# A fused attention and two feed-forwards: token chunks of 512, 384, 512, 512, 384 columns instead of 512 and four of 448, a 96-byte pad first on SBUF's right side, and attention paced anew

## The chip, the cores and the metric

One core of a Trainium2 chip. The time is that of the device for one execution, in microseconds. Five engines work side by side: TensorE (PE, matmuls; PEld is its weight load), VectorE (DVE), ScalarE (ACT), GpSimd (POOL) and SyncE (SP, which issues the DMAs).

## The reference

Attention over 4 batches, 8 heads, 576 positions of 64; heads 0 to 3 look at a window of 32 positions, heads 4 to 7 at every 32nd position. Then a feed-forward with a gate (512 to 1536 and back), then a second one that takes the largest of three products (512 to 768 and back).

```python
mask_local = (rel >= 0) & (rel < 32)
mask_strided = (rel >= 0) & (pos[None, :] % 32 == pos[:, None] % 32)
scores = np.where(masks, q @ k.T / np.sqrt(64), -1e9)       # heads 0-3 local, 4-7 strided
attn = np.exp(scores - scores.max(-1)); attn /= attn.sum(-1) + 1e-9
x = (attn @ v)                                              # 2304 tokens x 512
g = x @ w_gate
x = (g * (1.0 / (1.0 + np.exp(-g))) * (x @ w_val)) @ w_out  # first feed-forward
out = np.maximum(np.maximum(x @ w1, x @ w2), x @ w3) @ w_out2
```

## The kernel before

The 2304 tokens are 72 rows of 32 positions (18 rows to a batch). `ROWS` cuts them into five chunks; a chunk's width is 32 times its rows, and `width(c)` is the number of columns of every matmul of the first feed-forward for it. Rows 16 and 17 come last (`ORDER`).

*First feed-forward.* For each chunk c and each f of 12 there is a slot: `emit_gate` (12 matmuls into `ps_g`, a Silu on ACT, L717), `emit_val` (12 into `ps_v`, the multiply `ht` on DVE, L724, then its high part `hh` on ACT, L730, and its low part `hl` on POOL, L734) and `emit_out` of the slot before (12 into `ps_y`). `product` (L696 to L700) multiplies fp32 as three passes of a high and a low part: 36 wide matmuls to a slot. `ps_g` and `ps_v` share two banks of the pool `gv`. The weights `w_v` and `w_o` are read again from DRAM for every chunk but the first (`reload`, three buffers each), `w_g` stays in SBUF.

*Attention.* A chunk's attention is done while the chunk before it is in the feed-forward. The local heads go through PE in blocks of 64 queries (`Block`: scores L390, softmax on DVE and ACT, transposes L459, outputs L501); two blocks are done as a pair (`scores_with`, `outputs_with`), each having claimed its banks with a tiny ACT instruction (`claimed`, L306). A row group that has no neighbour in the chunk is a block with a single one. The strided heads of batch 0 (16 rows) and of batch 1's first 14 rows (`ON_PE`) go through PE as well (`strided_block`); the other rows are a `Unit` on DVE: a product over all keys and a sum (L597, L600) for each row's scores, exp on ACT (L607), a product and a sum for its outputs (L619, L622), and transposes on PE (L629). `attention_steps(c)` lays a chunk's attention out in 15 steps, which are called in the slots from three before to eleven after the beginning of chunk c - 1 (L1067 to L1072); a `Unit` takes four steps.

*Second feed-forward's weights.* In 60 steps (`pair_steps`, L256) the weights of the second feed-forward are loaded, rounded, combined and written to DRAM in the form in which they are used, with work on ACT, DVE and POOL. `PACE[c]` says how many of these steps a slot of chunk c takes, in the first ten slots of a chunk.

*Order of the work.* Chunk 0's feed-forward and chunk 1's attention are put in order by hand (`FIRST`: a letter for the kind of step, a number for the block, weight or f). From chunk 1 to slot 9 of chunk 4 the scheduler of the tile framework orders the instructions of each engine, and each engine works in that order. From slot 10 of chunk 4 on (the seam) the order is that of the code again: the loads and splits of `y` for the second feed-forward (`load_y`, `some`), the last two slots, and then the second feed-forward (L855), whose matmuls have 384 columns.

*SBUF.* The pools of the left side (`x`, `h`, weights, four of the second feed-forward's five weight buffers) and those of the right side (attention's tiles, `raw`, the strided keys and products; later `y`, its combinations `r` and one weight buffer) grow from both ends. In this kernel the tiles of the right side begin 96 bytes past a multiple of 128; those of the left side at multiples of 128.

Of the kernel before, what the change touches and what calls it, by code (L numbers as in the profile page):

```python
# [64 lines left out]
u4 B4 d14 V10 w4 c15 r20 s15 c16 t15 q16 s16 h14 y12 d15 P10 a17 o14 q17 O3 x4 c17 H10 l12 h15 t16 r23 s17 L10
z4 d16 E11 y13 o15 G5 h16 j4 q18 R11 m12 l13 m13 o16 a18 r24 s18 N11 t17 c18 a19 T11 d17 S12 u5 y15 t18 c19 B5
V11 w5 h17 M12 q19 r22 o17 a20 d18 E12 t19 s20 P11 y16 x5 G6 c20 h18 R12 H11 t20 z5 N12 s19 L11 r26 j5 q20 T12
o18 a21 O4 d20 r25 V12 d19 q21 h20 c21 h19 o20 r27 s21 t21 P12 S13 o19 a22 B6 d21 H12 l14 l15 u6 c22 L12 y19
h21 s22 w6 q22 o21 q23 r28 t22 O5 a24 x6 s23 c24 m14 m15 d22 z6 y18 q24 s24 h22 j6 a23 o22 G7 r29 a25 M13 c23
q25 t24 E13 r31 t23 c25 d24 W14 s25 d23 y21 B7 h24 R13 M14 h23 N13 u7 y22 o23 E14 w7 t25 T13 M15 r32 a26 o24  # L70
O6 V13 R14 s26 x7 q26 c26 r30 a27 N14 z7 t26 q27 d25 P13 r33 a28 j7 G8 h25 d26 H13 o25 s27 L13 c27 y24 h26 c28
t27 a29 T14 o26 q29 r34 B8 d27 V14 s28 u8 s29 c29 w8 y25 t28 h27 q28 t29 o27 a30 O7 r35 x8 s30 q30 d28 z8 y27
c30 h28 j8 a31 o28 q31 G9 d29 q32 y28 s31 c31 t30 h29 t31 E15 d30 O8 d31 u9 o29 h30 R15 h31 o30 a32 N15 y30
a33 w9 B9 s32 q33 o31 a34 c32 y31 q34 c33 s33 t32 T15 a35 x9 c34 G10 V15 t33 s34 z9 d32 q35 j9 h32 d33 s35 P14
# [1176 lines left out]
```

## Time and profile before

| | |
|---|---|
| time, median of 3 runs | 789.13 us (787.82 to 789.27) |
| profiled execution: span | 789.6 us |
| PE / DVE / ACT / POOL busy | 774.2 (98%) / 612.6 (78%) / 400.7 (51%) / 229.8 us (29%) |
| chunk 0 (25.90 to 143.40) | 117.50 us, DVE busy 110.48 |
| chunk 1 (143.40 to 240.30) | 96.90 us, DVE busy 78.04 |
| chunk 2 (240.30 to 336.50) | 96.20 us, DVE busy 88.03 |
| chunk 3 (336.50 to 430.20) | 93.70 us, DVE busy 84.02 |
| chunk 4 (430.20 to 518.00) | 87.80 us, DVE busy 64.91 |
| second feed-forward (518.00 to 789.60) | 271.60 us, DVE busy 172.58 |

The profile is of one execution. Busy times are sums of the durations of an engine's instructions in a stretch; an engine that is busy for the whole of one sets its length, if what it does is needed. The rows are in the section after the next. Line numbers are those of the kernel before; in the changed one the lines from L121 on stand two further down, those behind `attention_steps` four.

### The profile page before, as it was taken

The page shows a single profiled execution, that of the slowest core. Times are in us where ns is not written, and L with a number is a line of the kernel's source. Part 1 is how long each engine was busy: PE and PEld are TensorE (multiplying, and loading weights), DVE is VectorE, ACT ScalarE, POOL GpSimd, SP SyncE. Part 2 cuts the span into 40 slices and gives each one's busy share as a digit, 9 for nine tenths or more (in the row PEclk, how much of TensorE's full clock was granted, in tenths as well). Part 3 has the DMA queues.
Part 4 walks back from the last instruction along what each step waited for, and adds up shares of the span by engine and source line. Part 5 has one row for each costly group of instructions (what it writes and reads, how often), then busy time and mean ns, then how long its engine had stood idle before and what let it go on. Part 6 is the DMA issues. An engine that isn't in the chain of part 4 may idle for free.

```text
span 789.6 us, 13321 instructions
## 1 busy us (share of the span) xinstructions
PE 774.2 (98%) x4642; PEld 712.0 (90%) x4642; DVE 612.6 (78%) x1206; ACT 400.7 (51%) x925; POOL 229.8 (29%) x225
## 2 busy tenths in 40 slices
PE   6899999999999999999999999999999999999998
PEld 4677788889898998988999999999999999999998
DVE  4899999888959999799795778745689377856683
ACT  6899998554553636545342645433245233443331
POOL 1533343012221432424242646521124011321120
PEclk9899999999999999999999999999999999999999
DMA  9998896977656886747788999996775976878722
GB/s 273 315 316 290 309 356 217 383 255 252 205 202 202 302 294 221 269 169 251 254 277 288 311 387 378 346 370 249 274 265 195 418 258 244 285 285 343 271 94 81
DMA packets 75595, 216.26 MB, mean 274 GB/s; under 512 B 8488, under 2 KB 42024, under 8 KB 70920
## 3 DMA queue, kind: packets, MB, share of 16 engines
q1 hardware_dynamic: 75528, 215.41, 76.9%
q8 instruction: 37, 0.61, 0.3%
q14 instruction: 30, 0.25, 0.1%
HBM read 171.34 MB, written 44.04 MB: 273 GB/s over the span
## 4 chain that ended last, share of the span: by engine, by line
PE 82%; DVE 12%; ACT 3%; issue 2%; DMA 1%; SPq 0%; DVEq 0%; ACTq 0%
PE ps_a L855 19%; PE ps_c L855 10%; PE ps_v L698 5%; PE ps_y L698 5%; PE ps_y L699 5%; PE ps_v L700 5%; PE ps_v L699 5%; PE ps_y L700 5%; PE ps_g L698 5%; PE ps_g L700 5%; PE ps_b L855 5%; PE ps_g L699 5%; DVE pr L619 2%; PE ps_a L501 1%; PE ps_a L459 1%
## 5 line engine op out<-in xcount | busy, mean ns | idle before, releaser
L734 POOL TENSOR_TENSOR hl<-ht,hh 128x448 fp32r<-128x448 f32 x47 | 61.0, 1297 | 213.6 <-ACT hh L730 194.8
L866 ACT ACTIVATE s<-ps_a 128x384 f32<-128x384 f32 x99 | 48.4, 489 | 135.0 <-PE ps_a L855 135.0
L698 PE MATMUL ps_v<-xh,w_v 128*128 128x448 f32 (+1 forms) x240 | 90.8, 378 | 0.9 <-DVE ht L724 0.7
L698 PE MATMUL ps_g<-xh,wh_g 128*128 128x448 f32 (+1 forms) x240 | 90.4, 377 | 0.0
L699 PE MATMUL ps_g<-xl,wh_g 128*128 128x448 f32 (+1 forms) x240 | 89.9, 375 | 0.4 <-DVE xl L519 0.4
L700 PE MATMUL ps_g<-xh,wl_g 128*128 128x448 f32 (+1 forms) x240 | 89.8, 374 | 0.0
L699 PE MATMUL ps_y<-hl,w_o 128*128 128x448 f32 (+1 forms) x240 | 89.6, 373 | 0.0
L700 PE MATMUL ps_y<-hh,w_o 128*128 128x448 f32 (+1 forms) x240 | 89.3, 372 | 0.0
L700 PE MATMUL ps_v<-xh,w_v 128*128 128x448 f32 (+1 forms) x240 | 89.2, 371 | 0.0
L699 PE MATMUL ps_v<-xl,w_v 128*128 128x448 f32 (+1 forms) x240 | 88.9, 370 | 0.0
L698 PE MATMUL ps_y<-hh,w_o 128*128 128x448 f32 (+1 forms) x240 | 83.6, 376 | 0.0
L730 ACT ACTIVATE hh<-ht 128x448 fp32r<-128x448 f32 (+1 forms) x60 | 35.2, 587 | 90.1 <-DVE ht L724 82.8
L805 POOL TENSOR_TENSOR rT<-t,rT 128x384 f32<-128x384 f32 x9 | 12.5, 1390 | 149.3 <-DVE rT L804 149.3
L855 PE MATMUL ps_a<-y0hT,wr 128*128 128x384 f32 x162 | 54.9, 339 | 0.0
L855 PE MATMUL ps_a<-y1hT,wr 128*128 128x384 f32 x162 | 54.5, 337 | 0.0
L698 PEld LDWEIGHTS ps_v<-xh,w_v 128*128 128x128 f32 x240 | 45.1, 188 | 7.0 <-DVE ht L724 1.3
L699 PEld LDWEIGHTS ps_g<-xl,wh_g 128*128 128x128 f32 x240 | 45.4, 189 | 5.5 <-DVE xl L519 0.7
L698 PEld LDWEIGHTS ps_g<-xh,wh_g 128*128 128x128 f32 x240 | 45.3, 189 | 5.6 <-DVE ht L757 0.3
L700 PEld LDWEIGHTS ps_g<-xh,wl_g 128*128 128x128 f32 x240 | 45.4, 189 | 5.1
L698 PEld LDWEIGHTS ps_y<-hh,w_o 128*128 128x128 f32 x240 | 45.1, 188 | 5.2
L897 DVE TENSOR_TENSOR s<-ps_c,s 128x384 f32<-128x384 f32 x36 | 20.0, 556 | 38.2 <-ACT s L866 32.5
L700 PEld LDWEIGHTS ps_y<-hh,w_o 128*128 128x128 f32 x240 | 45.1, 188 | 5.1 <-DVE w_o L248 0.3
(256 smaller groups left out, 2102.1 us busy)
## 6 DMA issues: line engine op xcount, KB each, us to landing
wr<-wsdr SPq DMA_DIRECT2D x36, 1792.0 KB, 8.3
raw<-in_w_dram SPq DMA_DIRECT2D x60, 512.0 KB, 6.8
w_v<-wvdr SPq DMA_DIRECT2D x48, 512.0 KB, 4.2
w_o<-wodr SPq DMA_DIRECT2D x48, 512.0 KB, 4.8
wsdr<-whi SPq DMA_DIRECT2D x36, 256.0 KB, 3.6
wvdr<-w_v SPq DMA_DIRECT2D x12, 512.0 KB, 4.5
wodr<-w_o SPq DMA_DIRECT2D x12, 512.0 KB, 6.1
wsdr<-w SPq DMA_DIRECT2D x24, 256.0 KB, 4.0
```

The source lines that it names most:

```text
L459: nc.tensor.transpose(ps[:sm.shape[2], g * 128:(g + 1) * 128], sm[:, g], ident)
L501: ins = nc.tensor.matmul(ps[j * D:(j + 1) * D, at:at + nq], v, p, start=True, stop=True).ins
L619: eng.tensor_tensor(pv, self.v[:, :, 0:i + 1], self.sc[:, r:r + 1, 0:i + 1].to_broadcast([128, D, i + 1]), ALU.mult)
L698: nc.tensor.matmul(ps, wh, xh, start=first, stop=False)
L699: nc.tensor.matmul(ps, wh, xl, start=False, stop=False)
L700: nc.tensor.matmul(ps, wl, xh, start=False, stop=last)
L730: return nc.scalar.activation(hs[c, f][0], t, AF.Copy).ins
L734: return eng.tensor_tensor(hl, t, f32(hh), ALU.subtract).ins
L805: nc.gpsimd.tensor_tensor(b12, self.raw["B22"], b12, ALU.subtract)
L855: nc.tensor.matmul(ps, w[:, c, a, ks], b, start=first and n == q == 0, stop=last and n == len(wts) - 1 and q == 2, skip_group_check=True,)
L866: nc.scalar.activation(s, ps, AF.Copy)
L897: nc.vector.tensor_tensor(s, ps, s, ALU.add)
```

## The change

Five edits: `ROWS` (chunk widths 512, 448, 448, 448, 448 become 512, 384, 512, 512, 384), `ON_PE` (batch 1's strided rows on PE are 12 instead of 14, so rows 12 and 13 become rows of a `Unit`), `PACE`, the pad, and `attention_steps`, in which a `Unit` of fewer than three rows takes one step instead of four where a chunk has more than three of them (chunk 3 only). `FIRST` is the same list with block 11 (a single local group) left out and the blocks behind it renumbered.

```diff
-PACE = [0, 0.7, 1.4, 1.4, 3.1]
+PACE = [0, 0.4, 1.6, 1.6, 2.6]
-ROWS = [0, 16, 30, 44, 58, 72]
+ROWS = [0, 16, 28, 44, 60, 72]
-ON_PE = [(0, 16, 4), (1, 14, 4)]
+ON_PE = [(0, 16, 4), (1, 12, 4)]
...
-t6 x1 c7 m9 a8 d6 q8 r11 T8 t7 c8 z1 G2 V8 d7 h6 y3 j1 h7 o6 a9 o7 q9 r14 P8 s8 a10 c9 S9 u2 t8 l10 l11 H8 B2
+t6 x1 c7 m9 a8 d6 q8 r11 T8 t7 c8 z1 G2 V8 d7 h6 y3 j1 h7 o6 a9 o7 q9 r14 P8 s8 a10 c9 S9 u2 t8 l10 H8 B2 s9 M9
...
     dram = pool("dram", 1, space=bass.MemoryType.DRAM)
+    nc.gpsimd.memset(pool("pad", 1, side="right").tile([128, 24], F32, name="pad"), 0.0)
...
         for u in units:
+            span = 1 if u.n < 3 and len(units) > 3 else 4
             steps[s0].append(u.load)
             steps[s0].append(u.begin)
             for r in range(u.n):
-                steps[s0 + (2 * r // u.n)].append(lambda u=u, r=r: u.qk(r, eng))
-            steps[s0 + 2].append(u.softmax)
+                steps[s0 + span // 2 * r // u.n].append(lambda u=u, r=r: u.qk(r, eng))
+            s1 = s0 + (span + 1) // 2
+            steps[s1].append(u.softmax)
             for r in range(u.n):
-                steps[s0 + 2 + (2 * r // u.n)].append(lambda u=u, r=r: u.pv(r, eng))
+                steps[s1 + span // 2 * r // u.n].append(lambda u=u, r=r: u.pv(r, eng))
             for r in range(0, u.n, 3):
-                steps[s0 + 5 + r // 3].append(lambda u=u, r=r: u.out(r))
-            s0 += 4
+                steps[s1 + (3 if span > 1 else 1) + r // 3].append(lambda u=u, r=r: u.out(r))
+            s0 += span
```

With the pad the tiles of the right side begin at multiples of 128 bytes; the pad itself is 96 bytes a partition. In numbers of instructions: PE has two transposes more and the same matmuls; DVE has eight instructions more (one each of L597, L600, L619 and L622 over 832 and over 896 elements); ACT has two table loads more (30 instead of 28).

The rows below are instructions of one engine in its order: line, operation, the tile written, the tiles read, and the shape. The first place is ACT at the start of chunk 1. `ysb` is the copy of chunk 0's last sums, L437 the exponentials (`sm`) of an attention pair, L717 a Silu (`ht`), L306 the claim of a bank (`ps_a`). Before:

```order
L780 ACTIVATE ysb<-ps_y 128x512 x2
L437 ACT_TABLE_LOAD
L437 ACTIVATE sm,stat<-sm,stat 128x96 x2
L717 ACT_TABLE_LOAD
L717 ACTIVATE ht<-ps_g 128x448
L437 ACT_TABLE_LOAD
L437 ACTIVATE sm,stat<-sm,stat 128x96 x2
L306 ACTIVATE ps_a<-mh 1x1
L437 ACTIVATE sm,stat<-sm,stat 128x96 x2
L306 ACTIVATE ps_a<-mh 1x1
```

The same place in the changed kernel:

```order
L784 ACTIVATE ysb<-ps_y 128x512 x2
L439 ACT_TABLE_LOAD
L439 ACTIVATE sm,stat<-sm,stat 128x96
L721 ACT_TABLE_LOAD
L721 ACTIVATE ht<-ps_g 128x384
L439 ACT_TABLE_LOAD
L439 ACTIVATE sm,stat<-sm,stat 128x96 x3
L308 ACTIVATE ps_a<-mh 1x1
L439 ACTIVATE sm,stat<-sm,stat 128x96 x4
L308 ACTIVATE ps_a<-mh 1x1
```

The exponentials ahead of the second claim are eight instead of six, and the Silu stands behind the first instead of behind the second.

The second place is DVE in chunk 2, up to the multiply `ht` of slot 3. L612 to L622 are a `Unit`'s outputs, L279 a weight's low part. Before, these are all of the instructions between the multiplies of slots 2 and 3:

```order
L724 SCALAR_TENSOR_TENSOR ht<-ht,ps_v 128x448
L612 TENSOR_TENSOR stsc<-stsc,ssum 128x108
L619 TENSOR_TENSOR pr<-stv,stsc 128x832
L619 TENSOR_TENSOR pr<-stv,stsc 128x896
L279 TENSOR_TENSOR w_2796<-w_2796,whi 128x512
L279 TENSOR_TENSOR s_3147<-s_3147,whi 128x512
L724 SCALAR_TENSOR_TENSOR ht<-ht,ps_v 128x448
```

In the changed kernel, the last eleven of 34 rows; L428, which fills 16 rows ahead of these, is the score reduction (L426 before), and L218, L226 (L216, L224 before) are steps of a weight's conversion:

```order
L624 TENSOR_REDUCE sto<-pr 128x64
L621 TENSOR_TENSOR pr<-stv,stsc 128x960
L218 TENSOR_SCALAR w_3279<-w_3279 128x512
L621 TENSOR_TENSOR pr<-stv,stsc 128x1024
L444 TENSOR_SCALAR stat<-stat 128x4
L624 TENSOR_REDUCE sto<-pr 128x64
L226 SCALAR_TENSOR_TENSOR w_3279<-w_3279,raw 128x512
L444 TENSOR_SCALAR stat<-stat 128x4
L624 TENSOR_REDUCE sto<-pr 128x64
L445 RECIPROCAL stat<-stat 128x4
L728 SCALAR_TENSOR_TENSOR ht<-ht,ps_v 128x512
```

Outputs of four rows, a pair's score reductions and two conversions now stand in one interval between two multiplies, where before there were five instructions.

The third place is DVE in the seam, up to the multiply of chunk 4's last slot. L804 to L807 are combinations of `y`, L175 the low parts of `y` or of a combination. Before:

```order
L807 TENSOR_TENSOR rT_5785<-y0lB_5763,rT_5783 128x384
L175 TENSOR_TENSOR y0lB_5763<-y0lB_5763,y0hB_5790 128x384
L724 SCALAR_TENSOR_TENSOR ht<-ht,ps_v 128x448
L175 TENSOR_TENSOR y0lT_5853<-rT_5785,y0hT_5852 128x384
L804 TENSOR_TENSOR rT_5856<-rT_5769,y1lB_5766 128x384
L806 TENSOR_TENSOR rT_5859<-y1lB_5772,rT_5856 128x384
L807 TENSOR_TENSOR rT_5861<-y1lB_5775,rT_5859 128x384
L175 TENSOR_TENSOR y1lB_5766<-y1lB_5766,y1hB_5863 128x384
L175 TENSOR_TENSOR y1lB_5775<-y1lB_5775,y1hB_5866 128x384
L724 SCALAR_TENSOR_TENSOR ht<-ht,ps_v 128x448
```

In the changed kernel, the rows from the fourth behind the multiply of slot 10 on:

```order
L177 TENSOR_TENSOR y0lT_5822<-rT_5804,y0hT_5821 128x384
L811 TENSOR_TENSOR rT_5809<-y0lB_5787,rT_5807 128x384
L177 TENSOR_TENSOR y0lB_5787<-y0lB_5787,y0hB_5814 128x384
L177 TENSOR_TENSOR y0lT_5818<-rT_5807,y0hT_5817 128x384
L177 TENSOR_TENSOR y0lT_5877<-rT_5809,y0hT_5876 128x384
L808 TENSOR_TENSOR rT_5880<-rT_5793,y1lB_5790 128x384
L810 TENSOR_TENSOR rT_5883<-y1lB_5796,rT_5880 128x384
L811 TENSOR_TENSOR rT_5885<-y1lB_5799,rT_5883 128x384
L177 TENSOR_TENSOR y1lB_5790<-y1lB_5790,y1hB_5887 128x384
L177 TENSOR_TENSOR y1lB_5799<-y1lB_5799,y1hB_5890 128x384
L728 SCALAR_TENSOR_TENSOR ht<-ht,ps_v 128x384
```

Thirteen instructions on `y` stand between the last two multiplies instead of six; seven of them stood ahead of slot 10's multiply before.

## Rows read from the trace of the kernel before

**Rows 1.** Top of the page: the span.

```profile
span 789.6 us, 13321 instructions
```

**Rows 2.** PE's waits: engine, line, releaser; us in total, times, longest.

```profile
PE ps_a L390 <- DMA raw<-in_st_dram: 6.8, 4, 4.0
...
PE ps_v L698 <- DVE ht L724: 0.7, 2, 0.4
```

**Rows 3.** Busy time by stretch, chunks 2, 3, 4: start:end length, engines, clock, DMA share, GB/s.

```profile
240.30:336.50 96.20, 95.81 (x574) 86.54 (x573) 88.03 (x182) 51.35 (x116) 30.72 (x29) 1.00 0.78 263
336.50:430.20 93.70, 93.43 (x534) 84.64 (x533) 84.02 (x130) 40.86 (x87) 30.59 (x27) 1.00 0.71 241
430.20:518.00 87.80, 87.80 (x435) 81.41 (x434) 64.91 (x87) 40.93 (x82) 45.52 (x42) 1.00 1.00 361
```

**Rows 4.** Timeline, chunk 2's slot 8, DVE and PE: start, us, instruction, [idle before].

```profile
314.88 0.62 DVE L724 SCALAR_TENSOR_TENSOR ht<-ht,ps_v 128x448 f32<-128x448 f32 x1
...
315.56 0.47 PE L698 MATMUL ps_v<-xh,w_v 128*128 128x448 f32 x1 [0.39 <-DVE ht L724]
```

**Rows 5.** The chain of waits, stretches of 512, 448 and 384 columns: start, us, what.

```profile
104.04 0.23 PE ps_y L698
...
106.32 0.23 PE ps_y L699
...
480.80 0.20 PE ps_y L698
...
488.10 0.20 PE ps_y L698
...
583.74 3.17 PE ps_a L855 x18
...
683.93 3.12 PE ps_a L855 x18
```

**Rows 6.** Timeline of ACT at the start of chunk 1.

```profile
154.12 0.60 ACT L780 ACTIVATE ysb<-ps_y 128x512 f32<-128x512 f32 x1 [1.58 <-PE ps_y L699]
...
160.76 0.15 ACT L306 ACTIVATE ps_a<-mh 1x1 f32<-1x1 f32 x1
...
161.58 0.15 ACT L306 ACTIVATE ps_a<-mh 1x1 f32<-1x1 f32 x1
```

**Rows 7.** Timeline of PE at the start of chunk 1.

```profile
153.92 0.39 PE L700 MATMUL ps_y<-hh,w_o 128*128 128x512 f32 x1
...
162.35 1.15 PE L501 MATMUL ps_a<-loct 96*64 96x64 f32 x32
```

**Rows 8.** Groups of DVE's instructions by form: busy us, mean ns of one.

```profile
L224 DVE SCALAR_TENSOR_TENSOR w<-w,raw 128x512 int32<-128x512 int32 x39 | 30.0, 776 | 3.0 <-POOL raw L210 1.9 <-DMA wsdr<-whi 0.6 <-POOL w L216 0.5
...
L216 DVE TENSOR_SCALAR w<-w 128x512 f32<-128x512 f32 x24 | 18.2, 762 | 7.6 <-ACT w L199 7.5
...
L426 DVE CUSTOM_DVE_ANT_0 sm<-ps_a,cst 128x96 f32<-128x96 f32 x56 | 10.6, 254 | 0.3 <-PE ps_a L390 0.3
...
L619 DVE TENSOR_TENSOR pr<-stv,stsc 128x896 f32<-128x896 f32 x2 | 3.1, 1562 | 0.0
...
L622 DVE TENSOR_REDUCE sto<-pr 128x64 f32<-128x896 f32 x2 | 2.2, 1077 | 0.0
...
L622 DVE TENSOR_REDUCE sto<-pr 128x64 f32<-128x832 f32 x2 | 2.0, 1012 | 0.0
```

**Rows 9.** DVE's waits, that for ACT's exponential of a Unit.

```profile
DVE ssum L609 <- ACT stsc L607: 5.2, 4, 1.5
```

**Rows 10.** Groups of ACT's instructions: the table load ahead of a Silu.

```profile
L717 ACT ACT_TABLE_LOAD x14 | 18.0, 1283 | 3.1 <-PE ps_g L700 2.9
```

**Rows 11.** Timeline of DVE in the seam.

```profile
501.51 0.55 DVE L804 TENSOR_TENSOR rT<-rT,y0lB 128x384 f32<-128x384 f32 x1
...
503.84 1.37 DVE L806 TENSOR_TENSOR rT<-y0lB,rT 128x384 f32<-128x384 f32 x1
```

More of the change, by code (lines that the diff above doesn't have):

```diff
@@ L60 @@
 E8 d3 G1 x0 r10 h3 t4 t5 z0 o3 q5 y1 d4 a6 j0 s5 B1 R8 s6 l9 h4 d5 u1 r13 o4 q7 h5 N8 q6 w1 c6 O0 r12 a7 o5 s7
-t6 x1 c7 m9 a8 d6 q8 r11 T8 t7 c8 z1 G2 V8 d7 h6 y3 j1 h7 o6 a9 o7 q9 r14 P8 s8 a10 c9 S9 u2 t8 l10 l11 H8 B2
-s9 M9 c10 y4 L8 a11 d8 E9 w2 c11 r15 t10 O1 x2 h8 q11 R9 m10 m11 o8 z2 N9 r17 q10 t9 s11 T9 j2 G3 s10 d9 r16
-t11 V9 d10 h9 d11 y7 a12 o9 h10 P9 h11 s12 B3 y6 u3 o10 H9 o11 q12 L9 c12 W10 a13 w3 y9 q13 c13 a14 t12 M10
-M11 s13 x3 c14 O2 r21 q14 s14 z3 t13 E10 d12 r18 d13 G4 j3 h12 R10 h13 r19 o12 a15 N10 q15 t14 y10 a16 T10 o13
@@ L65 @@
[L65 to L74, printed above, removed]
@@ L75 @@
-P15 o32 u10 B10 t34 h33 w10 c35 H14 H15 d34 L14 L15 h34 o33 O9 o34 y33 x10 t35 z10 d35 y34 j10 h35 G11 o35 y35
-O10 u11 w11 B11 x11 z11 j11
+t6 x1 c7 m9 a8 d6 q8 r11 T8 t7 c8 z1 G2 V8 d7 h6 y3 j1 h7 o6 a9 o7 q9 r14 P8 s8 a10 c9 S9 u2 t8 l10 H8 B2 s9 M9
+c10 y4 L8 a11 d8 E9 w2 c11 r15 t10 O1 x2 h8 q11 R9 m10 o8 z2 N9 r17 q10 t9 s11 T9 j2 G3 s10 d9 r16 t11 V9 d10 h9
+d11 y7 a12 o9 h10 P9 h11 s12 B3 y6 u3 o10 H9 o11 q12 L9 c12 S10 a13 w3 y9 q13 c13 a14 t12 M10 s13 x3 c14 O2 r21
+q14 s14 z3 t13 E10 d12 r18 d13 G4 j3 h12 R10 h13 r19 o12 a15 N10 q15 t14 y10 a16 T10 o13 u4 B4 d14 V10 w4 c15
@@ new lines @@
+r20 s15 c16 t15 q16 s16 h14 y12 d15 P10 a17 o14 q17 O3 x4 c17 H10 l11 h15 t16 r23 s17 L10 z4 d16 y13 o15 G5 h16
+j4 q18 m11 l12 m12 o16 a18 r24 s18 t17 c18 a19 d17 S11 u5 y15 t18 c19 B5 w5 h17 M11 q19 r22 o17 a20 d18 E11 t19
+s20 y16 x5 G6 c20 h18 R11 t20 z5 N11 s19 r26 j5 q20 T11 o18 a21 O4 d20 r25 V11 d19 q21 h20 c21 h19 o20 r27 s21
+t21 P11 S12 o19 a22 B6 d21 H11 l13 l14 u6 c22 L11 y19 h21 s22 w6 q22 o21 q23 r28 t22 O5 a24 x6 s23 c24 m13 m14
+d22 z6 y18 q24 s24 h22 j6 a23 o22 G7 r29 a25 M12 c23 q25 t24 E12 r31 t23 c25 d24 W13 s25 d23 y21 B7 h24 R12 M13
@@ new lines @@
+h23 N12 u7 y22 o23 E13 w7 t25 T12 M14 r32 a26 o24 O6 V12 R13 s26 x7 q26 c26 r30 a27 N13 z7 t26 q27 d25 P12 r33
+a28 j7 G8 h25 d26 H12 o25 s27 L12 c27 y24 h26 c28 t27 a29 T13 o26 q29 r34 B8 d27 V13 s28 u8 s29 c29 w8 y25 t28
+h27 q28 t29 o27 a30 O7 r35 x8 s30 q30 d28 z8 y27 c30 h28 j8 a31 o28 q31 G9 d29 q32 y28 s31 c31 t30 h29 t31 E14
+d30 O8 d31 u9 o29 h30 R14 h31 o30 a32 N14 y30 a33 w9 B9 s32 q33 o31 a34 c32 y31 q34 c33 s33 t32 T14 a35 x9 c34
+G10 V14 t33 s34 z9 d32 q35 j9 h32 d33 s35 P13 P14 o32 u10 B10 t34 h33 w10 c35 H13 H14 d34 L13 L14 h34 o33 O9 o34
@@ L77 @@
+y33 x10 t35 z10 d35 y34 j10 h35 G11 o35 y35 O10 u11 w11 B11 x11 z11 j11
 """
```

## The prediction

> **What bounds the kernel now.** I read the top of the page first: the profiled span is 789.6 us, half a microsecond over the median of the runs (789.13), so I sum against 789.6 and take 0.5 off at the end [rows 1]. Next came what TensorE (PE) waited for: 6.8 us for the first input, before anything can start, and after that almost nothing. The one stall in the feed-forward that touches this change is `ps_v` waiting for the multiply `ht` on VectorE (DVE), L724: 0.7 us in two waits [rows 2]. So the time is the sum of PE's wide matmuls, and anything that changes their pace counts in full. The third view is the busy time by stage. PE fills chunks 2, 3 and 4 (95.81 of 96.20, 93.43 of 93.70, 87.80 of 87.80 us), but DVE is busy for 88.03 of the 96.20 us of chunk 2 and 84.02 of the 93.70 of chunk 3, and in chunk 4 the DMA engines are full (share 1.00, 361 GB/s) [rows 3]. The reader is to see that PE never waits and that two resources stand just behind it. How near shows in chunk 2's slot 8: the multiply starts at 314.88, and the next `ps_v` matmul starts at 315.56 after 0.39 us of idling for it [rows 4]. There the margin is used up already.
>
> **Part 1: other widths, the same tokens.** The two feed-forward chunk groups run 1728 matmuls of 448 columns before; after, 864 of 512 and 864 of 384. The chain gives the pace. At 512 columns ten steps take 106.32 - 104.04 = 2.28 us, 228 ns each; at 448, 36 steps take 488.10 - 480.80 = 7.30 us, 202.8 ns each; at 384, in the second feed-forward, 18 take 3.17 or 3.12 us, 176.1 or 173.3 ns [rows 5]. With 175.7 between the last two: 1728 x 202.8 = 350.4 us; 864 x 228 + 864 x 175.7 = 348.8. Chunk 4, which has hardly any small matmuls, gives 87.80 / 432 = 203.2 ns over the whole of it [rows 3], and so 351.1 us; the difference of -2.3 us is the one that I take. Ends: 173.3 for 384 gives -4.4; 228 ns being a rounded ten-step figure, 2 ns more at 512 gives +0.3.
>
> **Part 2: the pad.** It moves every tile of SBUF's right side to a multiple of 128 bytes. In the feed-forwards PE reads there only `y` and one of five weight buffers of the second one; `x`, `h` and the other weights lie left and stay. The nearest rows are the two stretches of 18 matmuls: 583.74 has `y` as its moving operand (right side), 683.93 has the second layer's `h` (left side): 176.1 against 173.3 ns [rows 5]. Over the 1134 matmuls that read `y`, the whole difference would be -3.2 us. The means over all of them differ by about 1 ns only, so I take -1.0, the end at zero being nearer; ends 0 and -3.2.
>
> The Trainium skill ("SBUF - State Buffer", Specifications (TRN2)) speaks against the pad: it gives SBUF 16-byte cachelines. 96 bytes is already a multiple of 16, so by that rule this part is worth 0; the 3.17 against 3.12 us of the rows neither proves nor excludes it.
>
> **Part 3: the start of chunk 1.** Here PE's work shrinks under a chain on ScalarE (ACT). The chain begins when chunk 0's last `ps_y` is done. PE starts that matmul at 153.92; ACT copies it out at 154.12, does six exponentials of an attention pair and one Silu among them, with table loads between, and claims the banks for the pair ahead with L306 at 160.76 and 161.58; PE enters L501 at 162.35 [rows 6, 7]. From the copy to the second claim's end (161.73) ACT is never idle: 7.6 us. PE fills that with 40 matmuls of 203 ns, 8.1 us, so it arrives 0.6 us after the claim. After, 36 matmuls of 175.7 ns stand there: 6.3 us. And the pair has eight exponentials instead of six (the odd row group is now a full pair): two cost 161.58 - 160.76 = 0.82 us together. PE would be at L501 8.1 - 6.3 = 1.8 us sooner and the claim 0.8 us later; 1.8 + 0.8 - 0.6 = 2.0 us of waiting. Ends: 0, if the claim got there by another route, and 2.4 with two more score reductions of 0.19 (10.6 / 56) ahead of the exponentials [rows 8]. I take 1.7, near the upper end, since every step of the chain has a row.
>
> **Part 4: DVE in chunks 2 and 3.** Batch 1's rows 12 and 13 leave PE's strided blocks and become products on DVE: eight more instructions of 832 and 896 elements, between 1.01 (L622) and 1.56 us (L619), 8.1 to 12.5 us [rows 8]. The cut at 60 instead of 58 also moves two rows of batch 3 ahead, and the table PACE gives chunk 2 16 weight steps for 14. I counted DVE's instructions between the last `ht` multiply of chunk 1 and that of chunk 2 in both programs: 2 more L597, 4 more L619, 6 more L622 (12 x 1.01 to 1.56 = 12 to 19 us), one more conversion (L216 0.76, L224 0.78, L228 about the same), two more L279 and four score reductions: 4 to 5 us. So 88.0 us becomes 104 to 112, say 107. PE's share of the same chunk grows by 432 matmuls x 25 ns = 10.8, from 95.8 to 106.6. DVE goes from 92% to full. What is late next: between the multiplies of slots 2 and 3 there stand 33 instructions, 15 us by the same rows, while PE needs 66 wide matmuls, 15.0 us, from the end of one `ps_v` to the start of the next but one, and the two multiplies themselves (0.62 each [rows 4]) come off that. DVE further waits in order for ACT's exponential in this kind of slot: 5.2 us in 4 waits, 1.5 the longest [rows 9]. Queued behind is everything on DVE, and PE waits through the multiply. In chunk 3's third slot the backlog shows on ACT: four exponentials wait for score reductions, which stand behind two products and two conversions on DVE, and the Silu that frees the next gate bank is queued behind three of them and a table load of 1.28 us [rows 10]. At full load, a slot can't win back what another lost. I put both places at 3.0 us together. Ends: 0 (products at 1.01, DVE at 104 of 106.6) and 8, since DVE idled for 8.2 us of chunk 2 before and at full load each such idle moment is PE's.
>
> Here the Trainium skill ("SBUF - State Buffer", Who interferes with whom) says that a DVE operation with two SBUF inputs and a GpSimd one shut each other out of a shared port for a whole instruction. The trace agrees: the product with two inputs over 896 elements takes 1562 ns (L619) where the reduction over the same 896 takes 1077 [rows 8]. GpSimd's `hl` gets wider in these very chunks; with every product at the slow end the part would be worth the 8.
>
> **Part 5: the seam.** Of the weight conversions, 24 instead of 25 remain for chunk 4, but paced at 2.6 a slot rather than 3.1 they end one slot later, and the slots are 36 x 27 ns = 1 us shorter. So the first splits of `y` slip: between the last two multiplies DVE now has 13 instructions where it had six. By the rows such a one takes 0.55 alone and 1.37 at the side of GpSimd [rows 11], so 7 to 11 us at 0.55 to 0.85 on average. PE gives 24 matmuls, then 12 of the sum and 6 of the second feed-forward before it needs `hh`: with the multiply and ACT's copy some 9.5 us against 8.7 to 12.4. I take 1.3; ends 0 and 2.9. Before, the stretch shows no stall.
>
> Attention on PE (two strided rows fewer in chunk 0, two transposes more later) comes to about zero. Reloads are equal in number and hidden.
>
> **Sum.** 789.6 - 2.3 - 1.0 + 1.7 + 3.0 + 1.3 = 792.3; less 0.5 is **791.8 us**.
>
> **Rivals.**
> *DVE keeps up everywhere, ACT's chain too.* For it: 0.7 us lost at 92% load is little [rows 2, 3]. Against: part 3 is arithmetic on one engine's unbroken chain. Then only pace and pad are left: 789.13 - 3.3 = 785.8, faster. It decides if the added products average below 1.05 us and chunk 1's claim is moved.
> *Half of it.* DVE stays just under full, so part 4 is zero, parts 3 and 5 come: 788.8, no change. For it: the lower ends of the rows.
> *Chunk 4 bound by its transfers.* 361 GB/s over 87.8 us is 31.7 MB; less one step (0.58 MB) still 86 us, against some 76 of PE. Loads run ahead of their use by the pools' three buffers, a slot (36 x 203 ns = 7.3 us) at the least; 2 to 8 us remain to be paid: 794 to 800. Against: loads may start in chunk 3, which has DMA to spare (0.71) [rows 3].
> *The pad does nothing.* As in part 2's lower end: 792.8. By the cacheline rule of the Trainium skill named there it would be this one.
>
> **Chances.** My forecast 0.43, the pad without effect 0.10, chunk 4 by transfers 0.07, half of it 0.19, all kept up 0.21. What a measurement here can tell from no change is about 0.2%, 1.6 us. So slower 0.60, same 0.19, faster 0.21. The forecast's own range, from the ends of the unknown costs, is 790 to 796.5; the whole one reaches down to the case where all is kept up and up to the mild end of the transfer case: 785.4 to 797.
>
> **What would show it.** In the changed profile: DVE near 107 us in chunk 2; PE waiting for `ht` in chunks 2 and 3, for L306 at the start of chunk 1, and in the last two slots of chunk 4; 18 matmuls on `y` in 3.12 to 3.15 us. If PE's waits after the start are still under 2 us, parts 3 to 5 are wrong and the time is near 786. If the gate bank waits for a weight `w_v`, transfers bind.

## The result, and the profile after

The changed kernel takes 799.22 us (median of 5 runs, 795.24 to 799.99) against 789.13 before; the ratio is 1.0117, 95% interval 1.0097 to 1.0138. It is slower, as forecast, but by 10 us and not by 2.7, and outside the range.

The profiled execution has a span of 795.6 us. Its stretches, in the columns of [rows 3]; first the start in the kernel before and in the changed one, since they differ by chance:

```profile
0.00:25.90 25.90, 16.22 (x241) 12.75 (x241) 14.57 (x97) 17.37 (x76) 5.94 (x14) 0.94 0.96 302
```

```profile
0.00:22.00 22.00, 13.37 (x236) 10.79 (x238) 13.83 (x97) 16.02 (x70) 5.19 (x14) 1.00 0.94 302
...
138.00:227.40 89.40, 87.25 (x602) 83.36 (x601) 79.54 (x175) 50.10 (x111) 14.87 (x17) 0.98 0.73 243
227.40:335.80 108.40, 106.06 (x586) 85.83 (x586) 104.80 (x208) 53.37 (x124) 38.06 (x34) 1.00 0.77 253
335.80:446.10 110.30, 107.31 (x522) 86.17 (x521) 84.75 (x124) 44.44 (x91) 34.26 (x29) 0.97 0.65 218
446.10:525.00 78.90, 77.04 (x440) 76.13 (x439) 57.19 (x81) 36.77 (x73) 41.06 (x40) 1.00 1.00 356
```

Chunk 2 is as loaded as forecast: DVE 104.80 us, PE 106.06. Two clock columns stand out, 0.98 in chunk 1 and 0.97 in chunk 3, where they were 1.00 before. The start tells nothing of the change: before, the granted clock was at its lower level there for 6.83 us (from 22.87 on), which cost some 3 us, and in this execution it wasn't; of the fourteen profiles of this case six have such a stretch at the start. So between the profiles some 9 us are to be explained behind it, not 6. That the medians lie 10.1 us apart is the choice of the executions: in every run for which both are known the span is 1.7 to 2.0 us shorter than the time, so the profiled execution before was one of about 791.4 us, above its median, and that of the changed kernel, with 797.58, lies below its own.

What PE waited for, in the form of [rows 2]:

```profile
PE ps_g L702 <- ACT ht L721: 2.9, 1, 2.9
PE ps_a L859 <- DVE y1lB L177: 1.9, 1, 1.9
...
PE ps_a L503 <- ACT ps_a L308: 1.7, 1, 1.7
PE ps_a L631 <- DVE xl L521: 1.5, 2, 1.3
PE ps_v L702 <- DVE ht L728: 1.3, 3, 0.5
...
PE ps_y L702 <- ACT hh L734: 0.9, 1, 0.9
...
PE ps_b L859 <- DVE ysb L782: 0.6, 1, 0.6
```

All but one are places that the prediction named: L503 is the start of chunk 1 (1.71 us at 156.58), `ps_v` stands in chunks 1 and 2, L631 (transposes of attention, which it had not named) in chunk 2, `ps_g` in chunk 3's third slot (2.90 at 367.17), and the `y1lB`, `hh` and `ysb` rows are the seam (1.86, 0.87, 0.65). Behind the start the waits sum to 12.2 us against 2.2 before. Now the same trace cut at the edges of the clock's lower level, in the columns of the stretches:

```profile
158.07:161.48 3.41, 3.41 (x13) 3.41 (x12) 2.11 (x7) 2.62 (x5) 1.21 (x1) 0.50 0.94 230
...
364.20:366.28 2.08, 0.07 (x1) 0.00 (x0) 1.77 (x8) 2.06 (x7) 0.00 (x0) 1.00 0.91 254
366.28:373.11 6.83, 5.94 (x16) 4.36 (x17) 3.77 (x8) 3.91 (x9) 1.87 (x2) 0.50 0.58 232
373.11:446.70 73.59, 73.59 (x344) 60.03 (x343) 52.31 (x69) 28.36 (x55) 25.80 (x23) 1.00 0.73 241
...
526.71:530.12 3.41, 3.41 (x12) 3.00 (x10) 2.74 (x5) 3.29 (x8) 2.54 (x3) 0.50 0.98 416
```

A clock column of 0.50 is the 1.2 GHz level, 1.00 is 2.4 GHz; a fall is a stretch at the lower one. PE stood still just before each of the three falls or at its beginning, and was busy for 12.76 of their 3.41 + 6.83 + 3.41 = 13.65 us. How slowly it worked there, two matmuls of 384 columns show that are seven steps apart:

```profile
527.46 0.52 PE L703 MATMUL ps_y<-hl,w_o 128*128 128x384 f32 x1
...
529.70 0.52 PE L704 MATMUL ps_y<-hh,w_o 128*128 128x384 f32 x1
```

That is 320 ns from start to start, against 173.9 elsewhere; with 512 columns it was 427 against 228.2. So 46% of the 12.76 us, 5.9 us, is lost. The prediction has no term for that.

The account of the two profiles: waits +10.0, clock behind waits +5.9, narrower and wider matmuls -3.7, the second feed-forward's pace -3.5: +8.7 us, and -3.0 for the clock at the start, which is chance: 5.7 against a measured 6.0.

### The profile page after: what moved, and what is told of

Same layout as the page of the kernel before. It is cut to its first block, busy times and chain, and to the rows that moved or that the text cites. A ratio compares the mean times of both kernels' runs of the same rounds, so it can differ in the third digit from the quotient of the medians.

```text
span 795.6 us, 13356 instructions
## 1 busy us (share of the span) xinstructions
PE 770.8 (97%) x4644; PEld 696.8 (88%) x4644; DVE 624.5 (78%) x1218; ACT 403.9 (51%) x928; POOL 229.8 (29%) x227
## 4 chain that ended last, share of the span: by engine, by line
PE 69%; DVE 18%; ACT 5%; DMA 4%; issue 2%; SPq 1%; POOL 1%; DVEq 0%; ACTq 0%; POOLq 0%
PE ps_a L859 19%; PE ps_c L859 9%; PE ps_b L859 5%; PE ps_y L702 4%; PE ps_y L704 4%; PE ps_y L703 4%; PE ps_v L702 4%; PE ps_g L702 4%; PE ps_v L704 4%; PE ps_v L703 4%; PE ps_g L703 4%; PE ps_g L704 4%; DVE pr L621 3%; DVE pr L599 2%; DVE stsc L602 2%
## 5 line engine op out<-in xcount | busy, mean ns | idle before, releaser
L738 POOL TENSOR_TENSOR hl<-ht,hh 128x512 fp32r<-128x512 f32 (+1 forms) x47 | 62.0, 1320 | 229.3 <-ACT hh L734 220.4
L702 PE MATMUL ps_g<-xh,wh_g 128*128 128x512 f32 (+1 forms) x240 | 90.7, 378 | 4.1 <-ACT ht L721 2.9
L702 PE MATMUL ps_v<-xh,w_v 128*128 128x512 f32 (+1 forms) x240 | 90.8, 378 | 1.3 <-DVE ht L728 1.3
L704 PE MATMUL ps_y<-hh,w_o 128*128 128x512 f32 (+1 forms) x240 | 90.1, 375 | 0.0
L703 PE MATMUL ps_y<-hl,w_o 128*128 128x512 f32 (+1 forms) x240 | 89.8, 374 | 0.0
L703 PE MATMUL ps_g<-xl,wh_g 128*128 128x512 f32 (+1 forms) x240 | 89.7, 374 | 0.1
L704 PE MATMUL ps_g<-xh,wl_g 128*128 128x512 f32 (+1 forms) x240 | 89.7, 374 | 0.0
L704 PE MATMUL ps_v<-xh,w_v 128*128 128x512 f32 (+1 forms) x240 | 89.2, 371 | 0.0
L703 PE MATMUL ps_v<-xl,w_v 128*128 128x512 f32 (+1 forms) x240 | 88.8, 370 | 0.0
L734 ACT ACTIVATE hh<-ht 128x512 fp32r<-128x512 f32 (+1 forms) x60 | 35.4, 590 | 102.3 <-DVE ht L728 90.1
L702 PE MATMUL ps_y<-hh,w_o 128*128 128x512 f32 (+1 forms) x240 | 85.8, 377 | 0.9 <-ACT hh L734 0.9
L702 PEld LDWEIGHTS ps_v<-xh,w_v 128*128 128x128 f32 x240 | 45.6, 190 | 8.6 <-DVE ht L728 2.9
L704 PEld LDWEIGHTS ps_v<-xh,w_v 128*128 128x128 f32 x240 | 45.3, 189 | 6.3 <-DVE w_v L250 0.5
```

Of the source, the lines that this page charges most:

```text
L702: nc.tensor.matmul(ps, wh, xh, start=first, stop=False)
L703: nc.tensor.matmul(ps, wh, xl, start=False, stop=False)
L704: nc.tensor.matmul(ps, wl, xh, start=False, stop=last)
L734: return nc.scalar.activation(hs[c, f][0], t, AF.Copy).ins
L738: return eng.tensor_tensor(hl, t, f32(hh), ALU.subtract).ins
```

## The experiments

Line numbers shift by a few where an edit adds lines.

**The pad alone.** The kernel before with the one added line.

```diff
     dram = pool("dram", 1, space=bass.MemoryType.DRAM)
+    nc.gpsimd.memset(pool("pad", 1, side="right").tile([128, 24], F32, name="pad"), 0.0)
```

> The kernel before with the 96-byte pad and nothing else. In the changed kernel's profile the second feed-forward's matmuls come every 173.4 ns against 175.7 before. Theory (the pad does that, by moving the right side's tiles to multiples of 128 bytes): 1512 x 2.2 ns = 3.4 us less, 785.7 us, with y at 173 to 174 ns in the profile. Rival (the pace differs from one execution to the next, or by the chunks' widths, and the pad does nothing): 789.1 us, y at 176 ns.

Measured 785.31 us (784.56 to 786.40, 6 runs), ratio 0.9952 (0.9937 to 0.9968): faster than both kernels. The stretch of the second feed-forward's last 1477 matmuls, of the kernel before and of this one:

```profile
526.60:789.00 262.40, 259.49 (x1477) 259.13 (x1475) 168.72 (x274) 91.83 (x202) 48.98 (x39) 1.00 0.67 252
```

```profile
525.00:784.00 259.00, 255.96 (x1477) 255.57 (x1475) 168.66 (x274) 91.91 (x202) 48.77 (x39) 1.00 0.68 255
```

3.4 us less with nothing else moved, and 18 matmuls (twelve on `y`, six on `h`) in 3.12 us, where they took 3.17 [rows 5]:

```profile
581.21 3.12 PE ps_a L856 x18
```

The pad does it, as the theory has it. But the matmuls on `h`, which lies left, got faster too (from 175.0 ns to 173.5, start to start; those on `y` from 176.0 to 173.3), so the place of the moving operand is not the whole of it. The code tells for each matmul which of the five weight buffers it reads. Of the matmuls on `y` in the kernel before, the 882 with weights from the left side took 176.7 ns, but the 252 with weights from the right side, which lie 96 bytes off like `y` itself, took 173.5. Here twelve of the first kind are followed by twelve of the second:

```profile
562.42 0.34 PE L855 MATMUL ps_a<-y0hB,wr 128*128 128x384 f32 x1
...
564.54 0.33 PE L855 MATMUL ps_a<-y0hT,wr 128*128 128x384 f32 x1
...
566.62 0.34 PE L855 MATMUL ps_a<-y0hT,wr 128*128 128x384 f32 x1
```

2.12 us, then 2.08. The matmuls on `h` took 173.7 ns in the one of three passes in which none of their weight buffers lies right, and 175.5 and 175.9 in the other two. So it was not a tile off the multiple of 128 that cost time, but two operands that lie differently to it; the pad puts them all alike.

**The change without the pad.**

```diff
-    nc.gpsimd.memset(pool("pad", 1, side="right").tile([128, 24], F32, name="pad"), 0.0)
```

> The changed kernel without the pad. Theory (pad worth 3.5 us, the rest of the change costs about 13.5 us): 802.5 to 803 us. Rival (pad worth nothing): 799.2 us.

804.50 us (803.32 to 806.10), ratio 1.0196 (1.0175 to 1.0217). 5.3 us above the changed kernel, some 2 more than the pad, and above what was expected; its profile has 255.2 instead of 251.8 us for the last 1452 matmuls of the second feed-forward, a fall of 10.24 us at the seam instead of 3.41, and a wait of 1.42 us in chunk 2 that was one of 0.38. The pad is a gain inside the change, and the rest costs some 14 us (799.22 against the 785.31 of the pad alone).

**The change with the old table of paces.**

```diff
-PACE = [0, 0.4, 1.6, 1.6, 2.6]
+PACE = [0, 0.7, 1.4, 1.4, 3.1]
```

> The changed kernel with the table PACE of before (0, 0.7, 1.4, 1.4, 3.1). In the changed kernel PE waits 2.9 us in chunk 3's third slot and 3.4 us at the seam, and the granted clock falls to 0.50 behind both (6.8 and 3.4 us long, 5.1 us lost). Theory (these two stalls come from the weight steps that the new table puts beside attention and later into the last slots; their cost is the wait and the clock together): seam back to the order of before, 5.1 us less; chunk 3's third slot with one weight conversion less ahead of the exponentials, up to 6.3 us less: 788 to 794 us. The 1.7 us at the start of chunk 1 stays. Rival (DVE is full because of the products that came from PE, whatever the pace): within 1.5 us of the changed kernel, 798 to 800 us, with the waits only moved.

790.73 us (789.65 to 792.16, 10 runs), ratio 1.0021 (1.0010 to 1.0033): 8.5 us less by four numbers. Its waits:

```profile
PE ps_v L702 <- DVE ht L728: 3.0, 2, 1.6
PE ps_g L702 <- ACT ht L721: 1.8, 1, 1.8
```

Chunk 3's 2.9 and the seam's waits are gone, but for one of 0.5, which is for a transfer (`w_o`). The 1.7 at the start of chunk 1 stays. The 1.8 and a 1.6 are new, in chunk 4, where 25 steps now fall into slots of 384 columns. No fall of the clock stands behind the start in this profile.

**The change with the old pace in chunk 4 alone.**

```diff
-PACE = [0, 0.4, 1.6, 1.6, 2.6]
+PACE = [0, 0.4, 1.6, 1.6, 3.1]
```

> The changed kernel with only chunk 4's entry of PACE as before (3.1 instead of 2.6). Theory (the seam's waits of 3.4 us and the clock's fall behind them, 1.7 us, come from conversions that end one slot too late): 794 us, with no PE wait over 0.6 us in the last two slots of chunk 4 and no fall of the clock there. Rival (the slots of 384 columns are too short for the splits of y anyway): 798.5 to 799.5 us, the wait still there. Chunk 3's wait of 2.9 us stays by both.

796.45 us (795.75 to 799.33), ratio 1.0100 (1.0077 to 1.0122): half-way between the two theories, and by the time alone not to be told from the changed kernel, whose interval overlaps. The waits tell more: the 1.86 is gone, 0.99 (`hh`) and 0.91 (`ysb`) stay without a fall, and so does chunk 3's 2.88. So conversions that end late are about half of the seam's 3.4 us. In chunk 2 a wait of 1.54 us has come, where the changed kernel had 0.38.

**Deliberate waits.** ACT repeats the copy that frees a bank at four places of the second feed-forward, in the kernel with the pad; a second kernel has the numbers the other way round.

```diff
+LATE = {(0, 1, 1): 14, (1, 0, 1): 17, (1, 2, 1): 21, (2, 1, 1): 27}
...
             self.s1 = snap(self.a, 1)
+            for _ in range(LATE.get((self.pgi), 0)):
+                nc.scalar.activation(self.s1, self.a, AF.Copy)
```

> The kernel before with the pad, in which ACT repeats the copy of ps_a to s1 14, 17, 21 and 27 times more in four groups of the second feed-forward, at some 0.4 us each, where PE has 18 matmuls (3.1 us) of other work before it needs the bank again. So PE gets deliberate waits of four sizes, from some 0.5 to 4 us and 7 to 8 us in sum, far from attention and from weight conversions. Theory (a wait of some 1.7 us and more often makes the granted clock fall to 0.50 for 3.4 or 6.8 us behind it, which costs half of that again): 785.3 + 7.5 + 3 to 7 = 796 to 800 us, with falls in the profile right behind the longest waits, and none behind those of a microsecond. Rival (the clock falls in the changed kernel had another cause, as chunk widths or DMA): the waits alone, 792.8 us, clock 1.0 throughout.

> The same with the four numbers of copies in the opposite order (27, 21, 17, 14). Theory: the falls of the clock go with the size of the wait and not with the place, so they stand behind the first two sites now; 796 to 800 us. Rival (place or time in the program decides): falls at the same places as in the kernel with the numbers the other way round, or none and 792.8 us.

832.29 us (830.19 to 833.20) and 831.27 (829.20 to 833.90), ratios 1.0549 (1.0529 to 1.0569) and 1.0544 (1.0513 to 1.0575). My sizes were too small: the waits came out at 6.33, 6.35, 10.05 and 13.19 us, 35.9 together (13.12, 8.44, 7.96, 6.40 in the other). The time is 47.0 us over the kernel with the pad alone, 1.31 for each microsecond waited. Each wait has its fall of the clock, of 6.8 to 13.7 us, and none stands anywhere else: they go with the waits. For the sizes of the changed kernel it needed a second try:

```diff
-LATE = {(0, 1, 1): 14, (1, 0, 1): 17, (1, 2, 1): 21, (2, 1, 1): 27}
+LATE = {(0, 1, 1): 4, (1, 0, 1): 6, (1, 2, 1): 8, (2, 1, 1): 10}
```

> The kernel before with the pad and fewer extra copies on ACT: 4, 6, 8 and 10 at the four places that had 14, 17, 21 and 27. There a wait grew by some 0.53 us with each copy from two copies on (6.33 us at 14, 13.19 at 27), so these should be about 1.0, 2.1, 3.1 and 4.2 us, the sizes that the changed kernel has, 10.4 us together. Theory (a wait of this size is followed by a fall of the granted clock in some executions, the longer the likelier; the four waits with 14 to 27 copies cost 47 us of time for 35.9 us of waiting, 1.31 each): 785.3 + 1.3 to 1.5 x 10.4 = 798.8 to 801 us; a fall behind the 3.1 and the 4.2, none behind the 1.0. Rival (falls need waits of 6 us; those of the changed kernel have another cause): 795.7 us and a clock of 1.0 behind all four.

799.31 us (797.70 to 800.62), ratio 1.0135 (1.0111 to 1.0158): 14.0 us for 9.3 us of waiting, 1.5 each. First the four matmuls with their waits in brackets, then the stretches behind the first and the third:

```profile
550.58 0.44 PE L857 MATMUL ps_a<-y0hT,wr 128*128 128x384 f32 x1 [1.10 <-ACT s L907]
...
617.03 0.44 PE L857 MATMUL ps_a<-y0hT,wr 128*128 128x384 f32 x1 [0.60 <-ACT s L907]
...
664.25 0.64 PE L857 MATMUL ps_a<-y0hT,wr 128*128 128x384 f32 x1 [3.27 <-ACT s L907]
...
735.97 0.67 PE L857 MATMUL ps_a<-y0hT,wr 128*128 128x384 f32 x1 [4.31 <-ACT s L907]
```

```profile
550.58:560.00 9.42, 9.42 (x54) 9.42 (x55) 7.78 (x12) 3.84 (x9) 2.31 (x2) 1.00 0.63 210
...
664.34:667.75 3.41, 3.41 (x11) 3.41 (x12) 2.76 (x4) 1.56 (x4) 1.15 (x1) 0.50 0.75 315
```

No fall follows the 1.10 and the 0.60: such a wait costs itself. The 3.27 costs 1.6 us more, since eleven matmuls behind it take 320 ns and not 173.4, and the 4.31 as much. That makes 3.2 of the 4.7 us beyond the waits; 0.8 is a wait in chunk 2 that was longer in this execution (1.89 against 1.10). There is no attention and no conversion of weights here, so that is shown apart from the change.

**Without the products that came to DVE.** In `qk` and `pv` of a `Unit`:

```diff
+            if self.b == 1 and i < 14:
+                return
             pr = pr_p[0].tile([128, NI * D], F32, name="pr")
...
+            if self.b == 1 and i < 14:
+                nc.gpsimd.memset(self.o[:, r], 0.0)
+                return
             pr = pr_p[0].tile([128, NI * D], F32, name="pr")
```

> The changed kernel without the eight products and sums that came to DVE (batch 1's rows 12 and 13 of the strided heads are not computed: their scores stay at the mask's value and their outputs are zero). Theory of the prediction (these eight, about 9.5 us of DVE, are what fills DVE up): the waits of chunk 2 (2.8 us with the small ones) and of chunk 3 (2.9 us and the clock's fall) go, some 6 to 8 us, 791 to 793 us. Rival (DVE's load as a whole is not it; the waits come from what stands ahead of one multiply or Silu in an engine's order: two weight conversions ahead of an attention pair's softmax): chunk 3's wait of 2.8 to 2.9 us and the seam's stay, 797 to 800 us.

802.39 us (799.51 to 805.46), ratio 1.0174 (1.0142 to 1.0207). Not faster at all:

```profile
PE ps_g L707 <- ACT ht L726: 5.1, 2, 2.9
PE ps_v L707 <- DVE ht L733: 3.3, 2, 2.8
```

Chunk 3's 2.9 is there as before, the seam's 1.9 too, and the scheduler, which arranges the rest anew, has made another of 2.8 in chunk 1 and one of 2.3 in chunk 2. So these eight are not what the waits hang on, and my theory falls. But the run is not a test of a full DVE in chunk 2: in the changed kernel the eight (9.2 us) stand at the beginning of chunk 1, from here to 168.7 us,

```profile
139.20 2.02 DVE L599 TENSOR_TENSOR pr<-stk,stq 128x832 f32<-128x832 f32 x2
```

and without them DVE is as busy in chunk 2 as with them (105.6 of 110.3 us against 104.8 of 108.4).

**The change with chunk 3's conversions out of its first three slots.**

```diff
-            due += PACE[c]
+            due += (16 / 7 if f > 2 else 0) if c == 3 else PACE[c]
```

> The changed kernel with chunk 3's 16 weight steps in its slots 3 to 9 instead of 0 to 9; all else as in the changed kernel. Theory (the 2.9 us wait in chunk 3's third slot is the two conversions that stand on DVE ahead of an attention pair's score reductions, and so hold the exponentials and the Silu behind them on ACT): the wait and the clock's fall behind it go (2.9 + 1.7 to 3.4 us), the rest stays: 792.9 to 794.6 us. Rival (DVE's backlog out of chunk 2 is the cause, the conversions are by the way): the wait of 2 to 3 us stays, in that slot or the next, 798 to 800 us.

794.92 us (791.70 to 798.16), ratio 1.0081 (1.0056 to 1.0106): 4.3 us less, a hair over the range. In the changed kernel DVE, ACT and PE do this around the third slot (their timelines, one fence each):

```profile
357.91 3.14 DVE L621 TENSOR_TENSOR pr<-stv,stsc 128x832 f32<-128x832 f32 x2
360.97 1.64 DVE L218 TENSOR_SCALAR w<-w 128x512 f32<-128x512 f32 x2
362.54 1.27 DVE L226 SCALAR_TENSOR_TENSOR w<-w,raw 128x512 int32<-128x512 int32 x2
363.74 0.24 DVE L428 CUSTOM_DVE_ANT_0 sm<-ps_a,cst 128x96 f32<-128x96 f32 x1
```

```profile
364.03 0.38 ACT L439 ACTIVATE sm<-sm,stat 128x96 f32<-128x96 f32 x1 [3.85 <-DVE stat L428]
...
365.23 1.28 ACT L721 ACT_TABLE_LOAD   x1
366.52 0.60 ACT L721 ACTIVATE ht<-ps_g 128x512 f32<-128x512 f32 x1
```

```profile
363.89 0.39 PE L704 MATMUL ps_y<-hh,w_o 128*128 128x512 f32 x1
367.17 0.80 PE L702 MATMUL ps_g<-xh,wh_g 128*128 128x512 f32 x1 [2.90 <-ACT ht L721]
```

The two conversions (2.8 us) stand on DVE between a Unit's products and the score reductions; ACT sits idle for 3.85 us until the first reduction, and the Silu that PE needs is queued behind the exponentials and a table load. With the conversions moved:

```profile
359.83 3.12 DVE L621 TENSOR_TENSOR pr<-stv,stsc 128x832 f32<-128x832 f32 x2
...
362.87 0.24 DVE L428 CUSTOM_DVE_ANT_0 sm<-ps_a,cst 128x96 f32<-128x96 f32 x1
```

The reductions follow the products at once, and PE has no wait there, though DVE comes out of chunk 2 as full as before (busy for 106.4 of 110.6 us) and has the same work in all. That is the cause of this wait: not how much DVE has to do, but what stands ahead of what. The trace shows it and not the time, whose interval still touches that of the changed kernel; a wait of 1.87 us in chunk 2, 0.38 in the changed kernel, takes part of the gain back.

**One more step of pace in chunk 3 than in the old table.**

```diff
-PACE = [0, 0.4, 1.6, 1.6, 2.6]
+PACE = [0, 0.7, 1.4, 1.6, 3.1]
```

> The changed kernel with PACE 0, 0.7, 1.4, 1.6, 3.1: chunks 1, 2 and 4 as in the table of before, chunk 3 as in the new one. With the whole old table (790.7 us) PE waits 1.6 and 1.8 us in chunk 4, where 25 steps are squeezed into slots of 384 columns, and 1.7, 1.4 and 1.5 us elsewhere. Theory (waits follow the conversions' places): with two steps more in chunk 3 the waits in chunk 4 go (3.4 us), those of chunks 1 and 2 stay (1.7, 1.4, 1.5 us), and chunk 3's wait of 2.9 us doesn't come back, since its conversions fall into other slots when chunks 1 and 2 hand over one step fewer: 787 to 788.5 us. Rival (1.6 steps a slot in chunk 3 is by itself what makes the 2.9 us there): 790.5 to 793 us.

787.52 us (785.38 to 789.11, 10 runs), ratio 0.9986 (0.9972 to 0.9999): within the forecast. Chunk 3 has 1.6 steps a slot, as in the changed kernel, and no wait: the conversions fall into other slots. And this is chunk 2:

```profile
230.60:337.40 106.80, 105.27 (x586) 85.97 (x585) 102.63 (x204) 52.77 (x121) 33.93 (x30) 1.00 0.70 233
```

DVE is busy for 96% of it, against 97% in the changed kernel, and the time is 11.7 us less: a full DVE does not by itself cost what the change cost. At 515.09 PE waits 0.40 us for a weight `w_v`, the prediction's sign for transfers that bind; so they are near there, but this is all that is to be seen of them.

**The pair beside chunk 1 two steps later**, on top of that table:

```diff
-        at = [0, 0, 4, 4, 8]
+        at = [0, 0, 6, 6, 10] if c == 2 else [0, 0, 4, 4, 8]
```

> The kernel with PACE 0, 0.7, 1.4, 1.6, 3.1 (787.5 us), in which the second attention pair that is done beside chunk 1 begins two steps later, so that its eight exponentials no longer stand ahead of the claim for the first pair's outputs. Theory (the 1.7 us wait at the start of chunk 1 is ACT's chain of exponentials ahead of the claim): that wait is gone from the profile; the pair's DVE work now falls into chunk 1's later slots, where waits of 1.4 us stand already, so the time gains between 0 and 2 us: 785.5 to 787.5. Rival (the wait is for chunk 0's last sums, or for the banks themselves): 1.7 us of waiting for L308 or its bank at the start of chunk 1 as before.

793.48 us (787.75 to 795.63, 12 runs), ratio 1.0046 (1.0026 to 1.0067). The wait for L308 is gone, which settles the chain of part 3; but the time rose by 6 us, and that I had not expected:

```profile
229.10 0.50 PE L702 MATMUL ps_g<-xh,wh_g 128*128 128x512 f32 x1 [1.52 <-ACT ht L721]
236.66 0.50 PE L702 MATMUL ps_g<-xh,wh_g 128*128 128x512 f32 x1 [1.60 <-ACT xh L642]
238.60 0.79 PE L703 MATMUL ps_g<-xl,wh_g 128*128 128x512 f32 x1 [1.20 <-DVE xl L643]
```

The late pair now holds up a Silu and the last rows of x for chunk 2: 4.3 us in three waits and a fall of 6.83 us. One wait was traded for three.

**Half of the widths, with the pad.** The kernel before with the pad, no other edit than

```diff
-PACE = [0, 0.7, 1.4, 1.4, 3.1]
+PACE = [0, 0.8, 1.4, 1.6, 3.1]
-ROWS = [0, 16, 30, 44, 58, 72]
+ROWS = [0, 16, 30, 46, 60, 72]
```

> The kernel before with the pad, of the other widths only half: chunks of 512, 448, 512, 448, 384 columns (ROWS 0, 16, 30, 46, 60, 72; the strided rows on PE, the order by hand and the Units' steps as before), and PACE 0, 0.8, 1.4, 1.6, 3.1. Measured paces: 203.2 ns at 448, 228.2 at 512, 173.9 at 384. Theory (the other widths gain by themselves, and cost only through waits that the order of DVE's and ACT's work puts on PE): 432 x (2 x 203.2 - 228.2 - 173.9) = 1.9 us less than the kernel with the pad alone (785.3), 783.4 us, plus what waits come in chunks 1 and 2, up to 2 us if they stay near a microsecond and no fall of the clock follows: 783.4 to 785.5. Rival (a chunk of 384 in the end, or any moved cut, brings waits of 1.5 us and more): 787 to 790 us.

786.49 us (785.06 to 789.81, 12 runs), ratio 0.9974 (0.9959 to 0.9990): not better than the pad alone. One wait of 1.97 us for `ht` in chunk 1, and a fall of 3.41 us behind it, take more than the 1.9 us back in the profiled execution. Of the twelve runs six have a mean clock of 1.000 and take 785.06 to 786.40 us, six one of 0.991 to 0.997 and take 786.57 to 789.81: the same program with and without falls.

## Why the prediction was wrong

The step that failed is the price of a wait. The sum put every wait down at its own length. A wait of 2 us and more is mostly followed by a stretch at 1.2 GHz, which in the changed kernel's profile cost 5.9 us beside 10 us of waits. The other terms were off too, but cancel, and that is luck: widths and pad gave 3.9 us more than the 3.3 put down, the waits took 4.0 more than the 6.0.

In the profiles of all these kernels, behind the start, a fall follows all seven single waits of 2.8 to 4.3 us, and three of sixteen of 1.5 to 2.3 us (waits within a few microseconds of each other, as at the seam, are not counted). The wait of 1.7 us for L308 stands in six profiles and has a fall behind it in two; so the price of such waits changes from one execution to the next. The mean clock of the runs agrees: 0.989 to 0.996 in the five of the changed kernel, 0.999 to 1.000 in the six with the pad alone. It will be a part of why the former are spread over 5 us and the latter over 2, but not the whole: 17 runs of the kernel before lie between 787.31 and 791.00. The trace of before could have warned me: its clock row of the start is below one, behind waits of 0.93, 0.63 and 0.96 us close together, and I read the clock column of the later stretches, all 1.00, as a constant.

The Trainium skill ("TensorE: Matmul & The Clock Gate", Why this matters for your kernels) says to leave no long idle gap between bursts of matmuls, or the clock drops. These runs agree for the long waits; they also show falls behind waits of 1.71, 1.72 and 1.97 us, of which that section does not speak, and there the measurement decides.

Point by point:

- *The base* (789.6, less 0.5): the half microsecond set a span beside a time, which in one and the same run are 1.7 to 2.0 us apart. It did no harm, since 791.8 is the median before and the sum of the differences, +2.7.
- *Other widths* (-2.3): right in sign, -3.7 by the paces measured. (Its upper end of +0.3 does not come out: 2 ns on 864 matmuls are 1.7 us, which leaves -0.6.) At 512 columns the pace was 228.2 ns as read. At 384 it is 173.9: here are ten steps from 152.80 to 154.54.

```profile
152.80 0.34 PE L703 MATMUL ps_g<-xl,wh_g 128*128 128x384 f32 x1
...
154.54 0.34 PE L704 MATMUL ps_g<-xh,wl_g 128*128 128x384 f32 x1
```

I had taken 175.7 from the second feed-forward, which the missing pad slowed.
- *The pad* (-1.0, ends 0 and -3.2): -3.5. The rows for it were there, 3.17 against 3.12 us [rows 5], though six of the first 18 matmuls are on `h`; I let means of single durations, which overlap, speak against a start-to-start time, which is what adds up. The rival by which it does nothing is refuted.
- *Start of chunk 1* (+1.7): 1.71. Both sides came as worked out from [rows 6, 7]:

```profile
148.28 0.60 ACT L784 ACTIVATE ysb<-ps_y 128x512 f32<-128x512 f32 x1 [1.58 <-PE ps_y L703]
...
156.39 0.15 ACT L308 ACTIVATE ps_a<-mh 1x1 f32<-1x1 f32 x1
```

```profile
156.58 1.15 PE L503 MATMUL ps_a<-loct 96*64 96x64 f32 x32 [1.71 <-ACT ps_a L308]
```

From the copy to the second claim 8.1 us, where it was 7.5, while PE was through in 6.3.
- *DVE in chunks 2 and 3* (+3.0): 5.2 us of waits (0.50, 0.38, 1.28, 0.19 and 2.90; 0.44 more in chunk 1), inside the ends. The places were right and the reason was not. The eight added products, with which the part begins, stand in chunk 1; chunk 2's load came as counted, from the rows that moved into it. The 2.9, more than half, goes without the conversions ahead of the reductions. The part had named these two conversions, and then priced the place by a full engine; the order of the work on it decides. What the waits of chunk 2 hang on was not tried by itself.
- *The seam* (+1.3, ends 0 and 2.9): 1.86 + 0.87 + 0.65 = 3.4. The part's own rows allow it: the 24, 12 and 6 matmuls that it counts for PE take 7.4 us at 175.7 ns, not 9.5, and against 7.4 its 8.7 to 12.4 leave 1.3 to 5.0. The splits of `y` came late as forecast, but they had also to wait for `y` itself, which I had taken to be there:

```profile
521.87 0.53 ACT L174 ACTIVATE y1hB<-y1lB 128x384 fp32r<-128x384 f32 x1 [1.52 <-DMA y1lB<-ydr]
...
523.58 0.47 ACT L721 ACTIVATE ht<-ps_g 128x384 f32<-128x384 f32 x1
```

Behind that transfer the last slot's Silu is queued. So something of the rival by which transfers bind chunk 4 was in it (DMA share 1.00 there), at the seam and not in the weights. How much of the 3.4 is the transfers' was not measured by itself; an earlier end of the conversions, which write to DRAM too, took about half.

The sum with measured sizes: 789.1 - 3.7 - 3.5 + 10.0 + 5.9 = 797.8, against 799.2. Waits and clock are those of one execution, and the five lie between 795.2 and 800.0, so the rest of 1.4 us stays open.
